# The last 96 hidden columns of a SwiGLU block: 64 of each weight in one product, 32 of each turned by DMA

## The chip, the cores and the metric

The kernel runs on one core of a Trainium2 chip. The core has a matrix engine (TensorE, PE in the profile, with its weight loads as PEld), VectorE (DVE), ScalarE (ACT), GpSimd (POOL) and a queue that issues DMAs (SyncE, SP); ScalarE's queue can issue DMAs too. The metric is device time in microseconds: the median of three runs of the kernel before is 252.13 us (251.43 to 252.75).

## The reference

The input x has 2048 tokens of 512 features, in bfloat16. Two branches are computed from it and mixed by a gate for each token:

```
g = sigmoid((x * gate_w).sum(-1))
a: q, k, v = x @ wqkv, 32 heads of 16; causal attention over the last 256 tokens; heads joined, @ wo
b: (silu(x @ w1) * (x @ w3)) @ w2            # w1, w3: 512 x 1376, w2: 1376 x 512
out = g * a + (1 - g) * b
```

The change is about branch b. Its hidden width is 1376 = 10 x 128 + 96, so that the last block of hidden columns is not full.

## The kernel before, in words

**Layout.** x lies turned in `xT` (features on partitions, four chunks of 128). Weights lie in `wqkv_sb`, `w1_sb`, `w3_sb`, `w2_sb` and `wo_sb`, loaded once. PSUM is used as one group of four banks, `su`, for attention scores and four single banks, `ch`, for everything else.

**Branch b.** For each of four blocks of 512 tokens (`tcb`) and each of eleven blocks of hidden columns (`f`, ten of 128 and one of 96), four products over the feature chunks give the gate part in one bank and four more the up part in another (`half`, L651). ScalarE takes the tanh of half the gate part (`th`, L656), VectorE makes from it, in two steps, silu(gate) times up (`m1`, L660 and `m2`, L665) and writes it to `hT`, hidden columns on partitions. Then for each of the block's four groups of 128 tokens eleven products with w2 (`part`, L702) give b, and VectorE scales it by 1 - g into `bsb` (`bev`, L707). The products stream 512 columns each; the block of 96 streams as many as a full one.

**Branch a.** For each quarter of the heads (`c`, 0 to 3) the projections (L374, L432) fill q, k and v; score batches (L493 near the diagonal, L525 and L533 far from it) go to `su`; ScalarE takes the exponential into `E` (L498, L540), VectorE and POOL mask it (L479, L552); p-v products of 34 columns (`pv`, L588) follow for each of 16 groups of tokens, VectorE normalises and gates them into `oc` (L596, L599), and a DMA issued by SP turns the tile into `OT` (`tr`, L605). When a group of tokens has all four quarters, four products with wo (`output`, L731) and one VectorE addition of `bsb` (L735) give the output, which SP stores (L740). The last group is done in two halves of 256 columns, the second stored from ScalarE's queue.

**Order.** The order is not written by hand. `Plan` holds every step with an engine, an assumed duration, what it depends on, the buffers it takes and frees, and a due time. `emit` goes through them as a list scheduler: it takes the engine that can start first, and of the steps that can start there at about the same time (a window of 0.005 us) the one with the earliest due time. `SLACK` is added to each step's end. Due times for attention come from `at(c, t)` with `T0` and `TA` and a lead for each kind; those of branch b are spread from `TF0` to `TF1` in proportion to the work; the output's are 8 us after `at(3, m)`. `landed` tells the planner when loads are there. The opening (`opening`, L255 to L282) is not planned: warm-up products, constants, and all loads in SP's queue, of which three times four turn x into `xT`. Each engine and each queue then carries out its own list in order, and waits at a step until what it needs is there.

**Names that the change touches.** `gw_turn` (L333) turns gate_w, which ScalarE's queue loads last into `gwr` (L264). `opening` and `constants4` set constants. `plan.pieces` splits a chain of four products into two steps, between which other work can be put.

## Time and profile before

| | |
|---|---|
| median of three runs | 252.13 us (251.43 to 252.75) |
| profiled execution, its own time | 251.68 us |
| its span, first to last instruction | 249.9 us |
| PE busy | 244.9 us (98%) |
| VectorE and ScalarE busy | 184.1 and 184.0 us (74%) |
| POOL busy | 107.4 us (43%) |
| products of the block of 96 (L651, 96 outputs) | 32 |
| turns of `oc` by DMA (L605) | 64, 2.3 us to landing (median) |

Groups carry the line of the kernel before. Durations of PE are modelled to the end of the pipeline, so one product of 512 columns is shown as 380 ns while the next starts 216 ns after it: what a stream costs is read from the chain in order of time, where pieces follow each other without overlap. SPq and ACTq rows are DMA issues; the time shown is that of the issue, not of the transfer. The granted TensorE clock was 1.00 in the whole execution.

### The profile page before, as it was taken

How to read it: one execution, taken by the hardware profiler on the slowest of the kernel's cores; microseconds unless marked ns; L12 is line 12 of the kernel's file. 1: busy time of each engine (PE TensorE's matmuls, PEld its weight loads, DVE VectorE, ACT ScalarE, POOL GpSimd, SP SyncE). 2: the span in 40 equal slices, each digit the busy share in tenths (PEclk: the TensorE clock that was granted, in tenths of full speed). 3: DMA queues.
4: the chain of work that ended last, by engine and by line, in shares of the span. 5: the costliest groups of instructions: out<-in, count | busy, mean ns of one | idle time of the engine just before them, and what ended most of it. 6: DMA issues, size and time to landing. Idle time of an engine off the chain costs nothing.

```text
span 249.9 us, 8005 instructions
## 1 busy us (share of the span) xinstructions
PE 244.9 (98%) x3434; PEld 132.9 (53%) x3434; DVE 184.1 (74%) x402; ACT 184.0 (74%) x181; POOL 107.4 (43%) x97
## 2 busy tenths in 40 slices
PE   7999999999999999999999999999999999999994
PEld 6545545555555455555455555545555546445452
DVE  5588978666877978775769887775669878786552
ACT  3579889687868988776788888766787774785521
POOL 7006560340808356391619174473538074150300
PEclk9999999999999999999999999999999999999999
DMA  7998950000000000000000000000000111111112
GB/s 212 314 266 253 221 116 18 13 5 13 8 18 6 13 14 11 16 8 13 5 18 13 13 7 13 14 11 13 8 18 26 55 29 54 34 50 32 50 34 68
DMA packets 28091, 13.14 MB, mean 53 GB/s; under 512 B 17336, under 2 KB 28056, under 8 KB 28056
## 3 DMA queue, kind: packets, MB, share of 16 engines
q1 hardware_dynamic: 27360, 12.17, 20.0%
q8 instruction: 27, 0.44, 0.8%
q10 hardware_dynamic: 696, 0.46, 0.6%
q14 instruction: 8, 0.07, 0.1%
HBM read 6.85 MB, written 2.10 MB: 36 GB/s over the span
## 4 chain that ended last, share of the span: by engine, by line
PE 93%; DMA 4%; DVE 1%; SPq 1%; issue 0%
PE ch L651 31%; PE ch L702 15%; PE ch L588 15%; PE ch L374 12%; PE su L493 8%; PE ch L432 6%; PE ch L731 5%; DMA OT<-oc 2%; PE su L525 2%; DMA w_sb<-in_B_w_dram 2%; DVE ot L735 1%; SPq L605 0%; DVE h L660 0%; SPq L249 0%; PE su L533 0%
## 5 line engine op out<-in xcount | busy, mean ns | idle before, releaser
L498 ACT ACTIVATE E<-su 128x2048 bf16<-128x2048 f32 x60 | 112.6, 1876 | 28.3 <-PE su L493 27.4
L552 POOL TENSOR_SCALAR_AFFINE_SELECT E<-E 64x1024 bf16<-64x1024 bf16 x56 | 65.1, 1162 | 119.2 <-ACT E L540 116.8
L651 PE MATMUL ch<-xT,w_sb 128*128 128x512 bf16 (+2 forms) x360 | 89.3, 375 | 0.4 <-DMA w_sb<-in_B_w_dram 0.4
L588 PEld LDWEIGHTS <-E 128*128 128x128 bf16 x1440 | 43.7, 96 | 12.3 <-issue 2.5
L651 PEld LDWEIGHTS <-w_sb 128*128 128x128 bf16 (+1 forms) x360 | 30.9, 99 | 31.0 <-issue 4.6
L588 PE MATMUL ch<-vbd,E 128*128 128x34 bf16 x1440 | 45.9, 178 | 0.0
L702 PE MATMUL ch<-w_sb,hT 128*128 128x512 bf16 (+1 forms) x176 | 44.0, 380 | 0.0
L479 DVE TENSOR_TENSOR E<-E,mdiag 128x512 bf16<-128x512 bf16 x64 | 33.7, 527 | 13.7 <-ACT E L498 13.3
L398 POOL TENSOR_SCALAR kbd<-kt,rowsA 128x512 bf16<-128x512 bf16 x24 | 37.5, 1573 | 6.8 <-DVE kt L395 5.5
L660 DVE SCALAR_TENSOR_TENSOR h<-tt,ch 128x512 bf16<-128x512 bf16 (+1 forms) x44 | 30.1, 685 | 12.6 <-ACT tt L656 12.0
L540 ACT ACTIVATE E<-su 128x2048 bf16<-128x2048 f32 (+1 forms) x16 | 26.6, 1663 | 12.6 <-PE su L525 7.9
L374 PE MATMUL ch<-xT,wqkv_sb 128*128 128x512 bf16 x128 | 34.1, 379 | 0.0
L665 DVE SCALAR_TENSOR_TENSOR hT<-h,ch 128x512 bf16<-128x512 bf16 (+1 forms) x44 | 30.2, 686 | 3.6
L656 ACT ACTIVATE tt<-ch 128x512 bf16<-128x512 f32 (+1 forms) x44 | 26.0, 594 | 6.8 <-PE ch L651 5.5
L599 DVE SCALAR_TENSOR_TENSOR oc<-ch,gq,rden 128x128 bf16<-128x128 f32 x64 | 22.4, 351 | 2.3
L493 PE MATMUL su<-qT,kbd 32*128 32x256 bf16 x480 | 23.9, 273 | 0.0
L702 PEld LDWEIGHTS <-hT 128*128 128x128 bf16 (+1 forms) x176 | 15.0, 97 | 16.3 <-issue 2.1
L596 DVE RECIPROCAL rden<-ch 128x8 f32<-128x8 f32 x64 | 13.1, 204 | 11.6 <-PE ch L588 10.7
L493 PEld LDWEIGHTS <-kbd 32*128 32x128 bf16 x480 | 7.1, 92 | 22.4 <-issue 21.8
L432 PEld LDWEIGHTS <-xT 128*128 128x128 bf16 x256 | 15.6, 97 | 4.6 <-issue 1.3
L731 PE MATMUL ch<-wo_sb,OT 128*128 128x512 bf16 (+1 forms) x68 | 16.6, 367 | 0.6 <-DMA OT<-oc 0.6
L374 PEld LDWEIGHTS <-wqkv_sb 128*128 128x128 bf16 x128 | 10.9, 97 | 11.3 <-issue 1.7
(54 smaller groups left out, 139.2 us busy)
## 6 DMA issues: line engine op xcount, KB each, us to landing
out_dram<-ot SPq DMA_DIRECT2D x15, 128.0 KB, 1.7
wqkv_sb<-in_A_wqkv_dram SPq DMA_DIRECT2D x6, 256.0 KB, 5.4
w_sb<-in_B_w_dram SPq DMA_DIRECT2D x1, 1280.0 KB, 6.5
w_sb<-in_B_w_dram SPq DMA_DIRECT2D x2, 608.0 KB, 5.9
w_sb<-in_B_w_dram SPq DMA_DIRECT2D x2, 512.0 KB, 5.5
OT<-oc SPq DMA_TRANSPOSE x64, 2.3
wo_sb<-in_A_wo_dram SPq DMA_DIRECT2D x1, 512.0 KB, 5.9
xs<-in_A_x_dram SPq DMA_DIRECT2D x1, 256.0 KB, 2.7
```

The costliest lines, as they stand in the source:

```text
L374: nc.tensor.matmul(pst[:], lhsT=wqkv_sb[:, dc, col + c * P:col + (c + 1) * P], rhs=xT[:, dc, tq * 512:(tq + 1) * 512], start=(dc == 0), st ...
L398: nc.gpsimd.tensor_scalar_mul(out=kv[:, :, h, :], in0=kt[kj.at["kt"]][:].rearrange("p (k t) -> p k t", t=KB), scalar1=rowsA[:, h:h + 1])
L432: nc.tensor.matmul(pst[:, mm * w:(mm + 1) * w], lhsT=xT[:, dc, m * P:(m + 1) * P], rhs=rhs, start=(dc == 0), stop=(dc == NDC - 1))
L479: nc.vector.tensor_tensor(out=e, in0=e, in1=mdiag[:, None, :].to_broadcast([P, 8, KB]), op=ALU.min)
L493: nc.tensor.matmul(su[:, s, par * 256:(par + 1) * 256], lhsT=kbd[r, 2 * t + par, :, :].rearrange("p a k -> p (a k)"), rhs=qT[r, q0:q0 + 25 ...
L498: nc.scalar.activation(out=E[ej.at["E"]][:, t % 4, :, :, 0:256], in_=su[:].rearrange("p s (a q) -> p s a q", a=2), func=ACT.Exp, scale=SCALE)
L552: nc.gpsimd.affine_select(out=e[lo:lo + KB], in_=e[lo:lo + KB], pattern=[[0, 16], [-1, KB]], compare_op=ALU.is_ge, fill=0.0, base=-1, chan ...
L588: nc.tensor.matmul(po[:, 34 * s:34 * s + 34], lhsT=e[:, off:off + P], rhs=vbd[:, 2 * t + par, s, :], start=(bi == 0), stop=(bi == len(bloc ...
L651: nc.tensor.matmul(ch[job.at["ch"]][0:fs, t0:t1], lhsT=w[:, dc, f * P:f * P + fs], rhs=xT[:, dc, tcb * 512 + t0:tcb * 512 + t1], start=(dc ...
L660: nc.vector.scalar_tensor_tensor(out=h1[job.at["h1"]][0:fs, :], in0=tt[job.at["tt"]][0:fs, :], scalar=1.0, in1=ch[job.at["ch"]][0:fs, :], ...
L665: nc.vector.scalar_tensor_tensor(out=hT[0:fs, f, :], in0=h1[job.at["h1"]][0:fs, :], scalar=0.5, in1=ch[up.at["ch"]][0:fs, :], op0=ALU.mult ...
L702: nc.tensor.matmul(bps[:], lhsT=hT[0:fs, f, mm * P:(mm + 1) * P], rhs=w2_sb[0:fs, f, :], start=(f == 0), stop=(f == NFC - 1))
```

## The change

**The 96 columns.** They are split into 64 and 32. For the 64, POOL copies w1's and w3's columns side by side into `wA`, and one chain of four products (`half` with `joint`) gives both gate and up, on partitions 0 to 63 and 64 to 127 of one bank. `th`, `m1` and `m2` then work on 64 partitions, with `m1` writing to the upper half.

For the 32, `wB` holds w1's and w3's columns, and `tail_columns` makes the products the other way round: tokens on partitions, x as the weight, 64 columns streamed, four chunks for each of four groups of 128 tokens, sixteen products. One tanh, and two VectorE steps over 4 x 32 columns, write the result into columns 64 to 95 of `hb`, which POOL has set to zero. Four DMAs on SP turn it, 128 x 128 each, into `hX`, so that the 32 columns come to lie on partitions 64 to 95. The joint block's `m2` waits for all four, and writes partitions 0 to 63 of `hX`; the value products read 96 partitions of it as the eleventh block. `hX` has two buffers, `hT` loses its eleventh block. `tail_columns` is put in ahead of the eighth of the eleven blocks.

**The end.** The output products of the last two groups of tokens are given as three products over the quarters 0 to 2 and one, later, over quarter 3. In the last half group, `bsb` is added on TensorE, by a product with the identity matrix, and ScalarE evicts the bank; the other half stays with VectorE.

**The plan.** `SLACK`, the window for equal starts, all due times and the assumed load times have other values. In the order as built, gate_w's turn stands on PE between the two halves of w1's first block, and both stand ahead of w3's; before, w3's first half came in between and gate_w's turn came after the second hidden block.

```diff
-SLACK = 0.08
+SLACK = 0.1039
...
-            rows = [r for r in lists[eng] if r[0] <= first + 0.005]
+            rows = [r for r in lists[eng] if r[0] <= first + 0.001]
...
+    FA = P // 2
+    FB = FL - FA
+    F0 = (NFC - 1) * P
...
-    hT = pp.tile([P, NFC, 512], BF16, name="hT")
+    hT = pp.tile([P, NFC - 1, 512], BF16, name="hT")
+    hX = pp.tile([P, 2, 512], BF16, name="hX")
+    wA = pp.tile([P, NDC, 2 * FA], BF16, name="wA")
+    wB = pp.tile([P, NDC, 2 * FB], BF16, name="wB")
+    tb = pp.tile([P, 4, FB], BF16, name="tb")
+    hb1 = pp.tile([P, 4, FB], BF16, name="hb1")
+    hb = pp.tile([P, 4, P], BF16, name="hb")
...
+        nc.gpsimd.memset(hb[:], 0.0)
...
-    T0, TA, TF0, TF1 = 10.0, 224.0, 0.0, 240.0
+    T0, TA, TF0, TF1 = 11.49, 234.3, -7.168, 250.6
...
-    landed = {"x": [4.0, 4.4, 15.6, 22.0, 30.0], "w13": [5.3, 5.8, 12.6, 19.8], "w2": 28.5,
-              "qkv": [6.6, 7.4, 8.2, 34.0], "wo": 31.5, "gw": 5.8}
+    landed = {"x": [3.7, 4.45, 15.4, 21.2, 30.2], "w13": [5.25, 6.15, 12.0, 18.7], "w2": 28.0,
+              "qkv": [7.1, 8.0, 8.8, 36.0], "wo": 32.0, "gw": 5.8}
...
-    a = add("PE", 0.1, gw_turn, [gw_in], 7.7, take=[(gjob, "ch")])
+    a = add("PE", 0.1, gw_turn, [gw_in], 9.407, take=[(gjob, "ch")])
...
-        lead = 18.0 if c else 3.0
+        lead = 9.235 if c else 0.5758
...
-        qdue = due if tq == 0 else at(c, 4 * tq - 4) - lead + 2.0
+        qdue = due if tq == 0 else at(c, 4 * tq - 4) - lead + 3.779
...
-        vdue = due + 1.5
+        vdue = due + 1.455
...
-        due = at(c, 4 * h) + 0.3
+        due = at(c, 4 * h) + 1.98
...
-        due = at(c, i) + -1.0
+        due = at(c, i) + 2.465
...
-    ffn_total = NTC * (NFC * 1.73 + 4 * 2.38)
+    ffn_total = NTC * ((NFC - 1) * 1.73 + 0.87 + 0.47 + 4 * 2.38)
...
+    w_ab = []
+    for dst, c0, src in ((wA, 0, w1_sb[:, :, F0:F0 + FA]), (wA, FA, w3_sb[:, :, F0:F0 + FA]),
+                         (wB, 0, w1_sb[:, :, F0 + FA:F]), (wB, FB, w3_sb[:, :, F0 + FA:F])):
+        def w_copy(dst=dst, c0=c0, src=src):
+            nc.gpsimd.tensor_copy(out=dst[:, :, c0:c0 + src.shape[2]], in_=src)
+
+        w_ab.append(add("POOL", 0.4, w_copy, [w13_in[3]], 22.0))
...
+        def tail_columns(tcb=tcb):
+
+            due = ffn_due(0.47)
+            job = Job()
+
+            def mm_b():
+                po = ch[job.at["ch"]]
+                for mm in range(4):
+                    m = 4 * tcb + mm
+                    for dc in range(NDC):
+                        nc.tensor.matmul(po[:, mm * 2 * FB:(mm + 1) * 2 * FB], lhsT=xT[:, dc, m * P:(m + 1) * P],
+                                         rhs=wB[:, dc, :], start=(dc == 0), stop=(dc == NDC - 1))
+
+            def cols(lo):
+                return ch[job.at["ch"]][:, 0:8 * FB].rearrange("p (m w) -> p m w", w=2 * FB)[:, :, lo:lo + FB]
+
+            def th_b():
+                nc.scalar.activation(out=tb[:], in_=cols(0), func=ACT.Tanh, scale=0.5)
+
+            def m1_b():
+                nc.vector.scalar_tensor_tensor(out=hb1[:], in0=tb[:], scalar=1.0, in1=cols(0),
+                                               op0=ALU.add, op1=ALU.mult)
+
+            def m2_b():
+                nc.vector.scalar_tensor_tensor(out=hb[:, :, FA:FL], in0=hb1[:], scalar=0.5, in1=cols(FB),
+                                               op0=ALU.mult, op1=ALU.mult)
+
+            a = add("PE", 0.47, mm_b, list(xt_ready[tcb]) + w_ab, due, take=[(job, "ch")])
+            a = add("ACT", 0.3, th_b, [a], due)
+            a = add("DVE", 0.25, m1_b, [a], due)
+            a = add("DVE", 0.25, m2_b, [a] + last_b, due, free=[(job, "ch")])
+            res = []
+            for mm in range(4):
+                def tr_b(mm=mm):
+                    nc.sync.dma_start_transpose(out=hX[:, tcb % 2, mm * P:(mm + 1) * P], in_=hb[:, mm, :])
+
+                res.append(add("SP", 1.1, tr_b, [a] + wx_done.get(tcb - 2, []), due, lat=1.3))
+            last_b[:] = res
+            return res
+
         for f in range(NFC):
-            fs = fsz(f)
-            due = ffn_due(1.73)
+            if f == NFC - 4:
+                turned = tail_columns()
+            joint = f == NFC - 1
+            due = ffn_due(0.87 if joint else 1.73)
             job = Job()
-
-            up = Job()
-
+            up = job if joint else Job()
...
+            def half(job, w, lo, hi, f=f, joint=joint, tcb=tcb, t0=0, t1=512):
                 for dc in range(lo, hi):
-                    nc.tensor.matmul(ch[job.at["ch"]][0:fs, t0:t1], lhsT=w[:, dc, f * P:f * P + fs],
+                    nc.tensor.matmul(ch[job.at["ch"]][:, t0:t1],
+                                     lhsT=wA[:, dc, :] if joint else w[:, dc, f * P:(f + 1) * P],
                                      rhs=xT[:, dc, tcb * 512 + t0:tcb * 512 + t1],
                                      start=(dc == 0), stop=(dc == NDC - 1))
 
...
+            rg = slice(0, FA if joint else P)
+            ru = slice(FA if joint else 0, P)
...
-            def m2(job=job, up=up, fs=fs, f=f):
-                nc.vector.scalar_tensor_tensor(out=hT[0:fs, f, :], in0=h1[job.at["h1"]][0:fs, :],
-                                               scalar=0.5, in1=ch[up.at["ch"]][0:fs, :],
+            def m2(job=job, up=up, rg=rg, ru=ru, f=f, joint=joint, tcb=tcb):
+                dst = hX[rg, tcb % 2, :] if joint else hT[:, f, :]
+                nc.vector.scalar_tensor_tensor(out=dst, in0=h1[job.at["h1"]][ru, :],
+                                               scalar=0.5, in1=ch[up.at["ch"]][ru, :],
                                                op0=ALU.mult, op1=ALU.mult)
...
-                                xt_ready[tcb] + win + last_up, due, [(job, "ch")])
-                b = plan.pieces(HALF, 0.2172, lambda lo, hi, half=half, up=up: half(up, w3_sb, lo, hi),
-                                [a], due, [(up, "ch")])
+                                xt_ready[tcb] + win + last_up + (w_ab if joint else []), due, [(job, "ch")])
+                b = a
+                if not joint:
+                    b = plan.pieces(HALF, 0.2172, lambda lo, hi, half=half, up=up: half(up, w3_sb, lo, hi),
+                                    [a], due, [(up, "ch")])
...
-            s1 = add("DVE", 0.69, m1, [t_], due, take=[(job, "h1")], free=[(job, "ch"), (job, "tt")])
-            s2 = add("DVE", 0.69, m2, [s1, b], due, take=[(hj, "hT")] if f == 0 else [],
-                     free=[(up, "ch"), (job, "h1")])
+            s1 = add("DVE", 0.69, m1, [t_], due, take=[(job, "h1")], free=[(job, "tt")] + ([] if joint else [(job, "ch")]))
+            s2 = add("DVE", 0.69, m2, [s1, b] + (turned if joint else []), due,
+                     take=[(hj, "hT")] if f == 0 else [], free=[(up, "ch"), (job, "h1")])
             if f:
                 s2.deps.append(hs[0])
             hs.append(s2)
...
+                    fs = P if f < NFC - 1 else FL
+                    ht = hT[:, f] if f < NFC - 1 else hX[0:FL, tcb % 2]
+                    nc.tensor.matmul(bps[:], lhsT=ht[:, mm * P:(mm + 1) * P],
                                      rhs=w2_sb[0:fs, f, :], start=(f == 0), stop=(f == NFC - 1))
...
-    def output(m, n0, n1, queue):
-        due = at(NDC - 1, m) + 8.0
+    def output(m, n0, n1, queue, late):
+        due = at(NDC - 1, m) + 19.44
         job = Job()
         part = n1 - n0
+        onto = queue == "ACT"
...
+        def onto_b():
+            nc.tensor.matmul(ch[job.at["ch"]][:, 0:part], lhsT=ident[:], rhs=bsb[:, m, n0:n1],
+                             start=False, stop=False)
+
         def oev():
-            nc.vector.tensor_tensor(out=ot[job.at["ot"]][:, 0:part], in0=ch[job.at["ch"]][:, 0:part],
-                                    in1=bsb[:, m, n0:n1], op=ALU.add)
+            dst = ot[job.at["ot"]][:, 0:part]
+            if onto:
+                nc.scalar.copy(out=dst, in_=ch[job.at["ch"]][:, 0:part])
+            else:
+                nc.vector.tensor_tensor(out=dst, in0=ch[job.at["ch"]][:, 0:part],
+                                        in1=bsb[:, m, n0:n1], op=ALU.add)
 
         def odma():
             eng = nc.sync if queue == "SP" else nc.scalar
             eng.dma_start(out=out2d[m * P:(m + 1) * P, n0:n1], in_=ot[job.at["ot"]][:, 0:part])
 
-        a = plan.pieces(HALF, 0.2172 * part / 512, omm, [ot_ready[(c, m)] for c in range(NDC)] + [wo_in], due,
-                        [(job, "ch")])
-        b = add("DVE", 0.69 * part / 512 + 0.02, oev, [a, b_ready[m]], due, take=[(job, "ot")],
-                free=[(job, "ch")])
+        each = 0.2172 * part / 512
+        if late:
+
+            a = add("PE", 3 * each, lambda: omm(0, NDC - 1),
+                    [ot_ready[(c, m)] for c in range(NDC - 1)] + [wo_in], due, take=[(job, "ch")])
+            if onto:
+                a = add("PE", each, onto_b, [a, b_ready[m]], due)
+            a = add("PE", each, lambda: omm(NDC - 1, NDC), [a, ot_ready[(NDC - 1, m)]], due)
+        else:
+            a = plan.pieces(HALF, each, omm, [ot_ready[(c, m)] for c in range(NDC)] + [wo_in], due,
+                            [(job, "ch")])
+        b = add("ACT" if onto else "DVE", 0.69 * part / 512 + 0.02, oev, [a] if onto else [a, b_ready[m]], due,
+                take=[(job, "ot")], free=[(job, "ch")])
         add(queue, 0.55, odma, [b], due, free=[(job, "ot")], lat=1.3)
 
     for m in range(NT - 1):
-        output(m, 0, D, "SP")
-    output(NT - 1, 0, D // 2, "SP")
-    output(NT - 1, D // 2, D, "ACT")
+        output(m, 0, D, "SP", m == NT - 2)
+    output(NT - 1, 0, D // 2, "SP", True)
+    output(NT - 1, D // 2, D, "ACT", True)
 
     with tc.manual_schedule():
         opening()
```

## The prediction

> **What bounds the kernel now.** I read first the page's busy times, then the chain that ended last, then the groups by shape, then PE's pieces in order of time.
>
> ```profile
> span 249.9 us, 8005 instructions
> PE 244.9 (98%) x3434; PEld 132.9 (53%) x3434; DVE 184.1 (74%) x402; ACT 184.0 (74%) x181; POOL 107.4 (43%) x97
> ...
> PE 93%; DMA 4%; DVE 1%; SPq 1%; issue 0%
> ```
>
> PE is busy all the time and carries 93% of the chain; VectorE and ScalarE have a quarter of the span free. A busy PE can hide gaps, so I priced the stream itself, from the chain in order of time:
>
> ```profile
> 7.60 1.73 PE ch L374 x8
> ...
> 44.09 0.59 PE ch L588 x24
> ...
> 64.70 0.89 PE ch L432 x16
> ...
> 240.29 1.20 PE ch L588 x48
> 241.49 0.89 PE ch L731 x4
> 242.40 0.70 DVE ot L735
> 243.10 0.64 SPq L605
> 243.84 2.32 DMA OT<-oc
> 246.21 0.73 PE ch L731 x5
> ```
>
> A product over 512 columns takes 1.73/8 = 216.2 ns, over 128 columns 0.89/16 = 55.6 ns, over 34 columns 0.59/24 = 24.6 ns. The first two lie on 1.9 ns + 0.418 ns per column (256: 109 ns, 64: 28.7 ns); 34 columns would be 16 ns by it, so 24.6 ns is a floor. A score batch (L493, L525) costs 0.43 us from stream to stream (in the timeline 0.33 from its first product to the next block's, and 0.1 ahead of it). Adding up PE's order of before with these prices, from 4.90 us on, puts the end of the last p-v product at 239.79 us; the profile has it at 241.49 us. The difference is nearly all in four places: 0.8 us at the opening, 0.25 near 26 us, 0.17 near 205 us, 0.5 near 226 us. So before is PE's sum plus about 1.7 us, and then a fixed tail of 8.4 us (241.49 to 249.9) set by the last turned tile: its DMA lands at 246.16, eight products of 256 columns follow, two additions, the store. The reader should see in the last five rows that at the end the chain leaves PE, and goes through the issue (SPq) and landing (DMA) of one turned tile.
>
> The opening, in the timeline (PE only waits there for w3's first columns), and SP's queue behind it:
>
> ```profile
> 2.00 0.62 ACTq L264 DMA_DIRECT2D gwr<-in_gate_w_dram  x1
> 5.14 0.60 PE L651 MATMUL ch<-xT,w_sb 128*128 128x256 bf16 x4
> 6.12 1.48 PE L651 MATMUL ch<-xT,w_sb 128*128 128x256 bf16 x12 [0.38 <-DMA w_sb<-in_B_w_dram]
> ```
> ```profile
> 29.03 2.05 SPq L605 DMA_TRANSPOSE OT<-oc  x1
> 31.18 1.18 SPq L605 DMA_TRANSPOSE OT<-oc  x1
> 32.45 1.18 SPq L605 DMA_TRANSPOSE OT<-oc  x1
> 33.73 2.36 SPq L605 DMA_TRANSPOSE OT<-oc  x1
> 36.18 1.18 SPq L605 DMA_TRANSPOSE OT<-oc  x1
> ```
>
> SP issues loads until 28.9 us; then the turns that have queued up go out one behind the other, 1.2 us each and now and then 2.05 to 2.4.
>
> **Products of the 96 columns.** Removed: per 512 tokens eight 512-column products (two blocks of 96 outputs); added: four such (64 columns of w1 and of w3 side by side) and sixteen of 64 columns. Over four blocks: 16 x 216.2 = 3.46 us off, 64 products on. The trace has none of 64 columns with a 128-column weight; the nearest rows bound one at 24.6 and 55.6 ns, 1.57 to 3.56 us in all. I take 28.7 ns, the line through the two longer rows, as it lies above the floor: 1.84 us. One 256-column product (bsb through the identity) adds 0.11. PE's sum: -3.46 + 1.84 + 0.11 = -1.51 us.
>
> Here a page speaks against the change. Every added product loads its own weight, and the PEld row has 97 ns for such a load (L432) while the stream advances 55.6 ns: loads overlap. The Trainium skill, "TensorE: Matmul & The Clock Gate", section "Back-to-back issue gap", gives a stream of load and product about 81 ns at 128 columns; the trace disagrees (55.6 ns), and its floor of about 25 ns for 1 to 64 columns agrees with 24.6. By 81 ns each the 64 would be 5.2 us and the whole sum +1.8 us.
>
> **VectorE, ScalarE, POOL.** Added: eight products-with-scalar over 128 columns on VectorE, which I bound by the reciprocal of 8 columns (0.20) and the 512-column row (0.69); I take 0.25: 2 us. ScalarE gets four tanh of 128 columns (0.17 to 0.59; 0.3 taken) and the last half eviction. POOL gets one memset (half of the 0.95 us one) and four copies at 22 us: 512 elements take 1.57 us there, so 256 and 128 take 0.8 and 0.4, 2.4 us together, done by about 21 us if w3's last columns land at 18.3 (issue 12.40 plus 5.9); their first reader on PE is due at about 24. All of it costs nothing while VectorE and ScalarE are a quarter idle; without that cover it would be 2 and 1.5 us.
>
> **Sixteen turns on SP.** In the built order the first chunk's four stand in SP's queue as 3rd, 4th, 5th and 7th behind the loads, that is behind 29.03 us. By the rows above they issue at 32.45, 33.73, 36.18 and about 38.7 (37.5 if no long issue falls among them), and a turn lands 2.3 us after issue: 39.8 to 41.0, or 42.3 with one more long issue. The second multiplication of the joint block (L732 of the changed file) waits for all four, and VectorE is in order: behind it stand a reciprocal and normalisation, a mask and a bsb scaling, and on PE the hX product and the value product that takes its bank. Its operands are ready at about 40.0 (joint product ends at 37.1, the exponential ahead of it on ScalarE at 38.5, tanh 0.6, mask and first multiplication 1.2), and PE reaches the hX product at 41.66, so a landing up to 40.9 is free. Bounds 0 to 1.5 us; I take 0.45. In the later chunks the turns have 11 to 16 us between the 64-column products and the joint block and cost nothing; in the fourth they stand ahead of the turn of p-v tile 5, which has 6.4 us until its output product: about 5.3 us of issues behind 203.5, then 2.3 to land, still covered by a microsecond. If it were not, PE would wait as it does at 226 us (0.5).
>
> **Opening.** gate_w's turn now stands ahead of the second half of w1's first block, and that half ahead of w3's. Four 256-column products (0.44) move into the wait that ends at 6.12. The landing of gwr is not in the trace: issued at 2.00, behind a load whose first reader starts at 5.14. If it lands by 5.7, -0.45; if it is the last to land, 0. I take -0.45, since 1 KB directly behind that load should follow it closely.
>
> **New order of the rest.** All due times change. Score batches stay 2.75 us or more apart in both orders (shortest 2.58 and 2.56 by the count), and p-v to output product is at least 4.0 us apart now against 3.4 to 3.6 before, where the waits at 205 and 226 us arose. I take these 0.67 us as gone. New waits elsewhere: the spacing shows none, and the bounds are 0 and 1.5 us (as many as before had); I take 0.
>
> **The end.** Of PE's -1.51, 1.2 us is work taken out from behind the last p-v product (3.8 instead of 4.97 us), where it only filled the wait for the turned tile; ahead of it the sum falls by 0.32. Behind the landing stand two 256-column products in place of eight, and the two halves are evicted side by side (ScalarE, VectorE) instead of in sequence: from 246.21 the last eviction ends after 0.8 instead of 1.17 us: -0.38. Two turns back to back took 2.13 and 1.19 us at 241.6; a short one would give another 1 us.
>
> **Sum** against the profiled execution (251.68 us: span 249.9 and 1.8 around it): -0.32 - 0.45 - 0.67 + 0.45 - 0.38 = -1.37, so 250.3 us. That execution was 0.45 us under the median of 252.13, so I forecast 250.8 us.
>
> **Rivals.**
> 1. The turns land in time and the last two issue quickly: another -0.45 and up to -1.0, 249.4 us. For it: most single turns issue in 1.09 us. Against: two of the four that took over 2 us are in SP's backlog, and one is the last but one. Chance 0.18.
> 2. The new order brings waits of its own of about 1 us: 251.8 us, no change to be told. For it: before had four such places. Against: PE's count shows no shortfall. Chance 0.17.
> 3. Slower: the first chunk's turns all issue at 2.36 us. The last is then issued at 43.5, lands at 45.8, the joint block's result is there at 46.5, PE stands 4.9 us: 252.13 - 1.82 + 4.9 = 255.2 us. It decides from a landing at 42.8 on, 1.9 us past the free point. Against it: the backlog's first five average 1.6 us. Chance 0.11.
> 4. The 64-column products run at the pace of their weight loads (97 ns each, 6.2 us, +4.4): 255.2 us. The 34-column stream at 24.6 ns with the same loads speaks against it. Chance 0.03. The Trainium skill's 81 ns ("TensorE: Matmul & The Clock Gate", section above) would give a milder form of it, +3.3 us and 254.1 us, and falls by the same rows.
>
> **How the numbers follow.** Forecast 0.51 (249.8 to 251.7), rivals 0.18, 0.17, 0.11, 0.03. Half a per cent, 1.26 us, is about what a measurement can tell from no change; the forecast lies just beyond it, so three quarters of its chance count as faster and one quarter as same, rival 1 as faster, rival 2 as same. Faster 0.56, same 0.29, slower 0.15. The range from 249.2 to 252.3 takes in forecast and rivals 1 and 2 and leaves out 3 and 4.
>
> **What would show it.** Right: 64-column products near 29 ns apart; joint second multiplication in the first chunk waiting under 1 us for a turn; the first f-block done by 7.1 us; last p-v product ending near 240.5; under 8.1 us from there to the end. Wrong: PE idle for microseconds at about 42 us, the 64-column products at 55 ns or more, or waits of PE in the new order that before did not have.

## The result

The changed kernel takes 251.25 us (median; 250.81 to 252.22), the kernel before, run beside it, 251.74 us. The ratio is 0.9974 [0.9962, 0.9986]: faster by a quarter of a per cent, half of what the prediction called measurable. The time lies 0.45 us above the forecast of 250.8 and inside its range, about midway between the forecast and rival 2 (251.8). That is not because the sum was right: it had a gain of 1.37 us, and the spans of the two profiled executions differ by 0.5. Four of its terms missed by 0.45 to 1.1 us each, in both directions, and 0.9 us of the misses did not cancel. The distance to the forecast is smaller than that because the forecast was taken from 252.13 us, three runs of the kernel before, which runs at 251.74 here; that is luck.

The profiled execution of the changed kernel took 251.17 us. The page:

```profile
span 249.4 us, 8138 instructions
PE 244.4 (98%) x3483; PEld 133.8 (54%) x3483; DVE 187.4 (75%) x409; ACT 185.4 (74%) x186; POOL 109.2 (44%) x102
...
PE 94%; DVE 2%; DMA 1%; ACT 1%; issue 0%; SPq 0%; DVEq 0%
```

PE is as busy as before, although work was taken from it. In the shares of the chain ScalarE's 1% is new, VectorE has gone from 1% to 2%, and DMA from 4% to 1%. The chain in order of time (start, length, what) says where:

```profile
4.11 1.71 PE ch L319 x16
...
93.43 1.89 ACT E L505
95.34 1.18 DVE E L486
96.52 0.61 DVE h L726
97.17 0.76 PE ch L595 x24
...
111.38 1.28 DVE E L486
...
142.45 0.45 PE ch L439 x8
142.91 0.47 PE ch L672 x16
...
243.63 2.23 DMA OT<-oc
```

Three things are to be seen. The first row is the turning of x at the opening: 16 products of 128 columns at 107 ns, twice the 55.6 ns that they take later (0.45/8 = 56 ns in the row at 142.45). At 93 to 97 and at 111 us the chain leaves PE for a mask of VectorE (L486), which lasts 1.2 to 1.3 us there; the same instruction takes 0.42 us in most places. And sixteen 64-column products (L672) take 0.47 us, 29 ns each.

The end, in the timeline:

```profile
240.69 1.36 PE L595 MATMUL ch<-vbd,E 128*128 128x34 bf16 x48
...
245.91 0.39 PE L804 MATMUL ch<-wo_sb,OT 128*128 128x256 bf16 x2 [0.28 <-DMA OT<-oc]
246.28 0.42 DVE L816 TENSOR_TENSOR ot<-ch,bsb 128x256 bf16<-128x256 f32 x1 [0.36 <-PE ch L804]
246.34 0.37 ACT L814 CAST ot<-ch 128x256 bf16<-128x256 f32 x1 [2.47 <-PE ch L804]
246.74 0.39 ACTq L821 DMA_DIRECT2D out_dram<-ot  x1
```

Before, five products stood behind the last turned tile, and the two halves were evicted one behind the other by VectorE:

```profile
246.21 0.72 PE L731 MATMUL ch<-wo_sb,OT 128*128 128x256 bf16 x5 [0.27 <-DMA OT<-oc]
...
246.58 0.81 DVE L735 TENSOR_TENSOR ot<-ch,bsb 128x256 bf16<-128x256 f32 x2 [0.24 <-PE ch L731]
```

Only two products of 256 columns stand there now, and the halves are evicted side by side.

The account between the two profiled executions uses PE's sum at the prediction's prices, laid against the real starts of the 76 score batches; where the distance between the two grows, PE waited. (The bracket of a timeline row gives about 0.3 us less for the same wait, because it starts at the modelled end of the product before.)

| | before | after | difference |
|---|---|---|---|
| PE's sum from 4.90 us to the last p-v product | | | -0.32 |
| distance at the first score batch (opening) | 0.79 | 1.25 | +0.46 |
| distance gained from there to the last batch (waits) | 1.03 | 1.46 | +0.43 |
| last p-v product's end to the end of the span | 8.4 | 7.35 | -1.05 |
| sum; the spans give 249.4 - 249.9 = -0.5 | | | -0.48 |

### The profile page after: what moved, and what is told of

It is laid out like the page before. It is cut to its first block, busy times and chain, and to the rows that moved or that the text cites. A ratio compares the mean times of both kernels' runs of the same rounds, so it can differ in the third digit from the quotient of the medians.

```text
span 249.4 us, 8138 instructions
## 1 busy us (share of the span) xinstructions
PE 244.4 (98%) x3483; PEld 133.8 (54%) x3483; DVE 187.4 (75%) x409; ACT 185.4 (74%) x186; POOL 109.2 (44%) x102
## 4 chain that ended last, share of the span: by engine, by line
PE 94%; DVE 2%; DMA 1%; ACT 1%; issue 0%; SPq 0%; DVEq 0%
PE ch L712 29%; PE ch L773 15%; PE ch L595 15%; PE ch L381 11%; PE su L500 8%; PE ch L439 6%; PE ch L804 5%; PE su L532 2%; PE su L260 1%; DVE E L486 1%; DMA OT<-oc 1%; PE ch L672 1%; ACT E L505 1%; PE ch L319 1%; DVE oc L606 0%
## 5 line engine op out<-in xcount | busy, mean ns | idle before, releaser
L505 ACT ACTIVATE E<-su 128x2048 bf16<-128x2048 f32 x60 | 112.6, 1877 | 28.7 <-PE su L500 27.8
L559 POOL TENSOR_SCALAR_AFFINE_SELECT E<-E 64x1024 bf16<-64x1024 bf16 x56 | 65.0, 1161 | 84.7 <-ACT E L547 82.3
L712 PE MATMUL ch<-xT,w_sb 128*128 128x512 bf16 (+1 forms) x328 | 79.5, 375 | 0.0
L405 POOL TENSOR_SCALAR kbd<-kt,rowsA 128x512 bf16<-128x512 bf16 x24 | 37.6, 1578 | 27.3 <-DVE kt L402 23.3
L595 PE MATMUL ch<-vbd,E 128*128 128x34 bf16 x1440 | 46.6, 178 | 0.5 <-DVE E L486 0.3
L712 PEld LDWEIGHTS <-w_sb 128*128 128x128 bf16 x328 | 28.3, 98 | 29.8 <-issue 3.6
L486 DVE TENSOR_TENSOR E<-E,mdiag 128x512 bf16<-128x512 bf16 x64 | 34.8, 544 | 9.1 <-ACT E L505 7.7
L773 PE MATMUL ch<-w_sb,hT 128*128 128x512 bf16 x160 | 41.3, 379 | 0.0
L726 DVE SCALAR_TENSOR_TENSOR h<-tt,ch 128x512 bf16<-128x512 bf16 (+1 forms) x44 | 30.1, 684 | 6.4 <-ACT tt L722 5.7
L732 DVE SCALAR_TENSOR_TENSOR hT<-h,ch 128x512 bf16<-128x512 bf16 x40 | 27.5, 687 | 3.8
L773 PEld LDWEIGHTS <-hT 128*128 128x128 bf16 x160 | 13.1, 97 | 13.0 <-issue 1.9
```

What stands on the lines that cost most here:

```text
L405: nc.gpsimd.tensor_scalar_mul(out=kv[:, :, h, :], in0=kt[kj.at["kt"]][:].rearrange("p (k t) -> p k t", t=KB), scalar1=rowsA[:, h:h + 1])
L486: nc.vector.tensor_tensor(out=e, in0=e, in1=mdiag[:, None, :].to_broadcast([P, 8, KB]), op=ALU.min)
L505: nc.scalar.activation(out=E[ej.at["E"]][:, t % 4, :, :, 0:256], in_=su[:].rearrange("p s (a q) -> p s a q", a=2), func=ACT.Exp, scale=SCALE)
L559: nc.gpsimd.affine_select(out=e[lo:lo + KB], in_=e[lo:lo + KB], pattern=[[0, 16], [-1, KB]], compare_op=ALU.is_ge, fill=0.0, base=-1, chan ...
L595: nc.tensor.matmul(po[:, 34 * s:34 * s + 34], lhsT=e[:, off:off + P], rhs=vbd[:, 2 * t + par, s, :], start=(bi == 0), stop=(bi == len(bloc ...
L712: nc.tensor.matmul(ch[job.at["ch"]][:, t0:t1], lhsT=wA[:, dc, :] if joint else w[:, dc, f * P:(f + 1) * P], rhs=xT[:, dc, tcb * 512 + t0:t ...
```

## Experiments

### Each part of the change alone

Theory A: the split of the 96 columns brings its gain by itself. Theory B: it is the order that the planner makes from it, with its new due times, that decides.

The first kernel has the split with the plan's numbers and the end as before:

```diff
-SLACK = 0.1039
+SLACK = 0.08
-    T0, TA, TF0, TF1 = 11.49, 234.3, -7.168, 250.6
+    T0, TA, TF0, TF1 = 10.0, 224.0, 0.0, 240.0
...   (all other due times, leads and load times too; output() as before)
```

> The 96 columns as in the changed kernel, but the plan's numbers and the output end as before. If the parts add up as the prediction has them, PE's stream loses 1.6 us and the time falls by 1.2 to 1.6 us against before, with the last p-v product that much earlier. If the gain of the split is given back by waits of whatever order the planner makes of it, the time falls by under 0.5 us and PE's idle places have grown by about a microsecond.

The second has the kernel before with the new end only (`output` with `late`, the addition of `bsb` on PE, ScalarE's eviction):

```diff
-    def output(m, n0, n1, queue):
+    def output(m, n0, n1, queue, late):
...
-    output(NT - 1, 0, D // 2, "SP")
-    output(NT - 1, D // 2, D, "ACT")
+    output(NT - 1, 0, D // 2, "SP", True)
+    output(NT - 1, D // 2, D, "ACT", True)
```

> Before with the output end of the changed kernel alone (last two groups in three and one products, last half added on TensorE and evicted by ScalarE; due times as before). By the prediction's working the stretch from the last landing to the end shortens by 0.38 us and PE's sum grows by 0.11: about -0.4 us. The rival, that the end is set by the issue and landing of the last turns alone, gives 0 to -0.1.

The third has the kernel before with the new numbers of the plan only:

```diff
-SLACK = 0.08
+SLACK = 0.1039
-    T0, TA, TF0, TF1 = 10.0, 224.0, 0.0, 240.0
+    T0, TA, TF0, TF1 = 11.49, 234.3, -7.168, 250.6
...   (and all other numbers of the change)
```

> Before with the plan's numbers of the changed kernel alone (slack, window, due times, assumed load times). By the prediction the opening gains 0.45 us and the waits near 205 and 226 us go (0.67): about -1 us. If instead the new order brings waits of its own (masks on VectorE that come late to a p-v product, seen at 97 and 112 us in the changed kernel) and the opening gains nothing when the matrix engine's clock comes late, it is 0 to +0.8 us.

The fourth is the changed kernel with the numbers of before, that is split and end together:

```diff
-SLACK = 0.1039
+SLACK = 0.08
...   (all numbers as in the first; output() as changed)
```

> The changed kernel with all of the plan's numbers as before. If the new numbers are worth the 1 us that the prediction gave them, this is slower than the changed kernel by about that, -0.4 to -0.8 us against before. If they cost what they bring or more, it is as fast as the changed kernel or faster: -0.7 to -1.6 us against before.

| split | end | plan | median, us | ratio to before |
|---|---|---|---|---|
| yes | no | no | 253.25 | 1.0056 [1.0026, 1.0085] |
| no | yes | no | 252.99 | 1.0028 [0.9999, 1.0056] |
| no | no | yes | 255.13 | 1.0123 [1.0082, 1.0164] |
| yes | yes | no | 252.70 | 1.0037 [1.001, 1.0064] |
| yes | no | yes | 251.29 | 0.9991 [0.9978, 1.0004] |
| yes | yes | yes | 251.25 | 0.9974 [0.9962, 0.9986] |

(The fifth row is the last but one experiment, below; end and plan without the split was not run.) No part alone gains, and the plan's numbers alone cost most; split and plan together have nearly the whole gain. For the split alone five of the twelve runs had a granted clock of 0.991 or 0.992 and took 254.1 to 254.6 us; the median of the other seven is 252.89 us, still slower than the kernel before beside it (251.93). The split takes 1.62 us out of PE's sum, as counted; in its order, PE's waits grow by 1.53 us at 39 and 0.55 us at 83 us, and from the last p-v product to the end it takes 9.6 us where the kernel before takes 8.4. The plan's numbers alone bring waits of 1.34, 0.84 and five of 0.4 to 0.6 us. All four kernels of the first four rows came out slower than either theory of their expectations had them.

The new end by itself shows a second effect. The timeline of that kernel:

```profile
246.65 0.28 PE L732 MATMUL ch<-wo_sb,OT 128*128 128x256 bf16 x1
246.77 0.81 PE L702 MATMUL ch<-w_sb,hT 128*128 128x512 bf16 x3
247.62 0.69 ACT L709 ACTIVATE bsb<-ch,omg 128x512 bf16<-128x512 f32 x1 [7.88 <-PE ch L702]
248.34 0.42 DVE L744 TENSOR_TENSOR ot<-ch,bsb 128x256 bf16<-128x256 f32 x1 [1.83 <-ACT bsb L709]
248.36 0.27 PE L736 MATMUL ch<-bsb,ident 128*128 128x256 bf16 x1 [0.78 <-ACT bsb L709]
```

The last turned tile is there at 246.6, but value products of branch b still stand on PE, and the eviction of the last group's `bsb` starts only at 247.62: b ends the kernel, not the turned tile. In the kernel before that eviction started at 244.78. The split with the old plan ends the same way, with the old end and with the new one. So with the old plan the new end doesn't set the end; which of the plan's new numbers it takes wasn't tried.

### Whose waits: POOL's far masks left out

In the changed kernel the two largest waits lie near 97 and 112 us. The timeline of the first:

```profile
92.70 4.83 POOL L559 TENSOR_SCALAR_AFFINE_SELECT E<-E 64x1024 bf16<-64x1024 bf16 x4 [1.25 <-ACT E L547]
...
95.34 1.18 DVE L486 TENSOR_TENSOR E<-E,mdiag 128x512 bf16<-128x512 bf16 x1 [0.70 <-ACT E L505]
...
96.44 0.67 DVE L726 SCALAR_TENSOR_TENSOR h<-tt,ch 128x512 bf16<-128x512 bf16 x1
...
97.17 0.76 PE L595 MATMUL ch<-vbd,E 128*128 128x34 bf16 x24 [0.23 <-DVE h L726]
```

While POOL works through four far masks (its masks on E, L559), VectorE's diagonal mask takes 1.18 instead of 0.42 us; the multiplication behind it in VectorE's list ends at 97.1, and PE's p-v product needs the bank that it frees. Theory: a mask that meets a POOL instruction is held up by it. Rival: it is slow or late for another reason, and the order alone makes the wait. Three kernels leave out POOL's far masks (and with them a part of the attention mask), with all orders kept:

```diff
-            for lo in (0, KB):
-                nc.gpsimd.affine_select(out=e[lo:lo + KB], in_=e[lo:lo + KB],
-                                        pattern=[[0, 16], [-1, KB]],
-                                        compare_op=ALU.is_ge, fill=0.0, base=-1, channel_multiplier=1)
+            return
```

On the changed kernel:

> The changed kernel, its order untouched, with POOL's far masks left out (part of the attention mask is then missing). Theory: VectorE's diagonal mask stands still while a POOL far mask runs (1.1 to 1.35 us in place of 0.42), VectorE's list slips, and PE waits for a mask or a bank: 0.6 us at 97 us and 0.45 at 112 us. Then the slow masks and those two waits go and the time falls by 0.9 to 1.2 us against the changed kernel (about -1.6 us against before). Rival: VectorE's list is too dense there whatever POOL does; then the waits stay and the time is that of the changed kernel.

On the split alone:

> The split of the 96 columns alone, in the order of the plan's numbers of before, with POOL's far masks left out. Theory: its waits of 1.5 us near 38 us and 0.55 us near 82 us, both behind a slow diagonal mask, go, and the gain of PE's sum comes through: 2 us less than with the far masks, about -0.7 us against before. Rival (the order is bad in itself, or the first chunk's turns set the wait): still +1 us or more against before.

On the kernel before, as control:

> Control: the kernel before with POOL's far masks left out. Its own waits (opening, 0.25 near 27 us, 0.5 near 227 us) stand behind DMAs, not behind masks, so theory expects 0 to -0.4 us. If leaving the far masks out takes as much here as in the two others, the masks cost every order the same and do not tell the orders apart.

| far masks left out of | median, us | ratio to before | waits of PE at these places |
|---|---|---|---|
| changed kernel | 249.91 | 0.9927 [0.9914, 0.9941] | both gone |
| split alone | 251.30 | 0.9974 [0.9963, 0.9986] | 1.53 falls to 0.88, 0.55 goes |
| kernel before | 251.61 | 0.9999 [0.9986, 1.0011] | (not there) |

VectorE's masks were nearly as slow in the kernel before. Its group, and that of the changed kernel (busy, mean ns, idle before):

```profile
L479 DVE TENSOR_TENSOR E<-E,mdiag 128x512 bf16<-128x512 bf16 x64 | 33.7, 527 | 13.7 <-ACT E L498 13.3
```
```profile
L486 DVE TENSOR_TENSOR E<-E,mdiag 128x512 bf16<-128x512 bf16 x64 | 34.8, 544 | 9.1 <-ACT E L505 7.7
```

Without far masks the mean is 436 ns in the first of the three kernels and 432 in the third. In the changed order leaving them out gains 1.3 us (251.25 to 249.91); in the order of before the ratio shows nothing. That nothing isn't quite one: the three kernels without far masks spend about 2.0 us outside the span from first to last instruction, all others 1.7 to 1.8. By the medians of the spans the gain is 1.65 us in the changed kernel (249.55 to 247.9) and 0.45 us in the kernel before (250.1 to 249.65), and by the count PE's waits fall to 0.15 us in both profiled executions, from 1.46 and 1.03. So leaving out the far masks gains in both orders, and over three times as much in the new one: how much a held-up mask costs depends on whether PE at once needs what stands behind it. For the split alone most of the loss goes too, but 0.88 us of the first wait stays.

### POOL's instructions in halves

Here the whole computation is kept; each far mask and each k mask of POOL (L405, which fills `kbd`) is issued as two of half the size, in the same order:

```diff
-            e = E[ej.at["E"]][:, 2 * i:2 * i + 2, :, :, 256:320].rearrange("p t s a q -> p (t s a) q")
             for lo in (0, KB):
-                nc.gpsimd.affine_select(out=e[lo:lo + KB], in_=e[lo:lo + KB],
-                                        pattern=[[0, 16], [-1, KB]],
-                                        compare_op=ALU.is_ge, fill=0.0, base=-1, channel_multiplier=1)
+                for t in (2 * i, 2 * i + 1):
+                    e = E[ej.at["E"]][:, t, :, :, 256:320].rearrange("p s a q -> p (s a) q")
+                    nc.gpsimd.affine_select(out=e[lo:lo + KB], in_=e[lo:lo + KB],
+                                            pattern=[[0, 8], [-1, KB]],
+                                            compare_op=ALU.is_ge, fill=0.0, base=-1, channel_multiplier=1)
...
+                for k0 in (0, 4):
                     nc.gpsimd.tensor_scalar_mul(
-                    out=kv[:, :, h, :], ...
+                        out=kv[:, k0:k0 + 4, h, :], ...
```

On the changed kernel:

> The changed kernel, its order untouched, with each POOL far mask and each POOL k mask done as two of half the size. If VectorE's mask stands still for as long as one POOL instruction lasts, no diagonal mask takes over about 1 us any more, the waits at 97 and 112 us shrink by half or go, and the time falls by 0.4 to 1.0 us against the changed kernel. If VectorE waits for the whole run of POOL work, or slows by sharing, nothing changes, or POOL's longer total (some 20 us more) costs time.

250.05 us, ratio 0.9921 [0.9905, 0.9937]. The same place in its timeline:

```profile
92.84 5.50 POOL L562 TENSOR_SCALAR_AFFINE_SELECT E<-E 64x512 bf16<-64x512 bf16 x8 [0.74 <-ACT E L549]
...
95.47 0.42 DVE L488 TENSOR_TENSOR E<-E,mdiag 128x512 bf16<-128x512 bf16 x1 [0.69 <-ACT E L507]
...
95.95 0.69 DVE L729 SCALAR_TENSOR_TENSOR h<-tt,ch 128x512 bf16<-128x512 bf16 x1
...
96.90 0.76 PE L598 MATMUL ch<-vbd,E 128*128 128x34 bf16 x24
```

The mask starts at nearly the same point beside the same run of POOL's masks, but 0.04 us ahead of one of the halves and no longer 0.23 us into a whole one; it takes 0.42 us, and PE waits for nothing. Over the whole kernel, by groups (busy, mean ns, idle before):

```profile
L562 POOL TENSOR_SCALAR_AFFINE_SELECT E<-E 64x512 bf16<-64x512 bf16 x112 | 74.0, 683 | 75.1 <-ACT E L549 64.4 <-PE ch L598 8.3
...
L488 DVE TENSOR_TENSOR E<-E,mdiag 128x512 bf16<-128x512 bf16 x64 | 28.8, 449 | 9.6 <-ACT E L507 8.2 <-ACT E L555 0.9
```

POOL pays 16 us more (109.2 to 125.0), 9 of them for the far masks (65.0 to 74.0, two times 683 ns for one of 1161), and no wait of PE leads to it; the masks' mean falls from 544 to 449 ns, and PE's waits by the count from 1.46 to 0.14 us. This kernel is faster than both others. Far masks and k masks were not halved one without the other.

On the kernel before, as control:

> The kernel before, with each far mask and each k mask of POOL as two instructions of half the size; orders of all engines unchanged. Theory A (a mask of VectorE that is blocked by a long POOL instruction costs time only where PE's next product waits for what stands behind it, and the order of before has no such place): ratio 0.998 to 1.001, 251.4 to 252.1 us, PE's waits at 26.8, 207 and 227 us as before. Theory B (shorter POOL instructions are worth what they were worth in the changed kernel whatever the order, 0.9974 to 0.9921): ratio about 0.995, 250.6 us.

251.06 us, ratio 0.9976 [0.9963, 0.9989]: between the two theories, nearer to theory A by the time, and against it by the waits. Halving helps before too, by half of what it gives the changed kernel; PE's waits, 1.03 us before, sum to 0.1. So the statement that before had no place where a held-up instruction costs time is too strong. The timeline of the kernel before shows such a place:

```profile
202.53 1.19 DVE L479 TENSOR_TENSOR E<-E,mdiag 128x512 bf16<-128x512 bf16 x1 [1.56 <-ACT E L498]
...
204.41 0.69 DVE L665 SCALAR_TENSOR_TENSOR hT<-h,ch 128x512 bf16<-128x512 bf16 x1
...
205.16 1.02 PE L651 MATMUL ch<-xT,w_sb 128*128 128x512 bf16 x4
```

The mask takes 1.19 us, the second multiplication behind it, which frees a bank, ends at 205.10, and PE's next products start at 205.16, 0.17 us late by the count. The wait of 0.25 us near 26 us stands in the same way behind a mask of 0.87 us (23.55). The one near 226 us stands behind a turned tile, which lands 3.54 us after its issue with the halves in place of 3.85; why is open. With halves on both sides the change is worth 1.0 us by the medians (251.06 - 250.05) and 1.4 us by the ratios (0.9921/0.9976 = 0.9945), about twice what it is worth without.

On the split alone:

> The split alone (the kernel of 253.25 us, ratio 1.0056, with waits of 1.53 us at 39.2 and 0.55 us at 82.7), with POOL's far masks and k masks in halves; whole computation kept. Theory A (both waits are VectorE's masks blocked by POOL's long instructions): both waits fall below 0.4 us, 251.0 to 251.6 us, ratio 0.9965 to 0.999. Theory B (the first wait comes from something else in VectorE's list, as 0.88 us of it stayed when the far masks were left out): about 0.9 us stays there, 251.7 to 252.2 us, ratio 0.999 to 1.001.

251.35 us, ratio 0.9977 [0.9959, 0.9996]: the time that theory A gave, but by the waits theory B holds for the first place. The second wait went; of the first, 1.28 of 1.53 us stayed, by the count. Its timeline:

```profile
33.89 1.88 ACT L507 ACTIVATE E<-su 128x2048 bf16<-128x2048 f32 x1 [0.37 <-PE su L502]
...
35.80 0.89 DVE L488 TENSOR_TENSOR E<-E,mdiag 128x512 bf16<-128x512 bf16 x1 [0.77 <-ACT E L507]
...
36.61 0.74 DVE L390 TENSOR_SCALAR kbd<-ch,rowsA 128x512 bf16<-128x512 f32 x1
...
37.27 0.67 DVE L729 SCALAR_TENSOR_TENSOR h<-tt,ch 128x512 bf16<-128x512 bf16 x1
...
38.00 0.76 PE L598 MATMUL ch<-vbd,E 128*128 128x34 bf16 x24 [0.99 <-DVE h L729]
```

The mask stands ahead of two steps that free banks, and VectorE waits 0.77 us for ScalarE's exponential before it; then all three run one behind the other while PE stands. This same mask takes 1.13 us in the split alone, 0.89 with the halves and 0.42 without far masks, and the bracket before the p-v product reads 1.24, 0.99 and 0.54 us: PE's wait changes by what the mask changes. So the held-up mask is 0.70 of the 1.24 us and the order the rest. My reading that both waits of the split alone are held-up masks was right for a little over half of this one.

### The end and the opening by themselves

The changed kernel with the end as it was:

```diff
-    def output(m, n0, n1, queue, late):
+    def output(m, n0, n1, queue):
...   (body and calls as before; due time 19.44 kept)
```

> The changed kernel with the end as it was before (eight products of the last half tile behind its turn, both additions on VectorE). Theory A (the prediction's end term): 0.38 us slower than the changed kernel, from the last landing to the last eviction 1.17 us in place of 0.80; 251.5 to 251.8 us, ratio 0.9985 to 1.0005. Theory B (the new end is worth nothing, as it was worth nothing when put into the kernel before by itself, 1.0028): 251.2 us, ratio 0.9974.

251.29 us, ratio 0.9991 [0.9978, 1.0004]. The medians put it 0.04 us from the changed kernel, the ratios 0.17% (0.4 us); the intervals overlap, and the time does not tell the theories apart. The timeline supports the mechanism: from the last turned tile's first product (245.74) to the end of the last eviction (246.93) it is 1.19 us, against 0.80 in the changed kernel (245.91 to 246.71). PE's start was 0.35 us earlier in this execution, which hides it in the span.

The changed kernel with w1, w3, w1, w3 at the opening, as before, and gate_w's turn behind them (the numbers are those of the plan's steps: 872 to 875 the block's halves, 25 and 26 gate_w's turn and its eviction, 876 the tanh):

```diff
+        was = [872, 25, 874, 26, 873, 876, 875]
+        new = [872, 873, 874, 875, 25, 26, 876]
+        at = {op.seq: n for n, (est, op) in enumerate(order)}
+        row = {op.seq: (est, op) for est, op in order}
+        for a, b in zip(was, new):
+            order[at[a]] = row[b]
         self.order = order
```

> The changed kernel with one edit in the opening: the first hidden block's halves in the order of before (w1, w3, w1, w3), gate_w's turn behind them; all else in the same order. Theory A (the prediction's opening term: w1's second half fills the wait for w3's first columns): 0.45 us slower than the changed kernel, 251.7 us, ratio 0.9992, and PE waits 0.3 to 0.5 us for w3 ahead of the second group of four products. Theory B (what the new order saves at w3 it gives back, since the first products run at half pace and w3 has landed by then, or since gate_w is waited for): 251.0 to 251.4 us, ratio 0.9965 to 0.998.

251.38 us, ratio 0.9993 [0.998, 1.0007]: by the medians it is 0.13 us slower than the changed kernel, as theory B has it, and by the ratio it is where theory A has it, so the time does not tell them apart. The timelines show why the gain can't be relied on. In this kernel PE waits for w3:

```profile
6.43 1.48 PE L718 MATMUL ch<-xT,w_sb 128*128 128x256 bf16 x12 [0.45 <-DMA w_sb<-in_B_w_dram]
```

and in the kernel with the plan's numbers alone, which has the new order, for gate_w, until much the same time:

```profile
6.30 0.17 PE L334 MATMUL ch<-ident,gwr 4*128 4x4 bf16 x1 [0.54 <-DMA gwr<-in_gate_w_dram]
```

In the changed kernel without far masks PE waits for gate_w until 6.22. So the new order trades one wait for another. And where the first products run slowly for long (the row of 16 products shown in the next section lasts 1.73 to 1.91 us in five of the 14 profiled executions, the changed kernel's among them) PE waits for neither load; in the other nine it waits 0.24 to 1.79 us for one of them.

## Why the prediction was right, and where it was wrong

**PE's sum: right.** 64-column products take 29.4 ns (0.47/16), against 28.7 taken and bounds of 24.6 and 55.6; no weight load shows in them. Rival 4 falls, in its milder form too. The split alone gives -1.62 us, and the whole change -1.51 us, by the count at these prices.

**VectorE, ScalarE, POOL at nothing: right for the added work, wrong in the reason.** The copies on POOL take 0.40 and 0.29 us, the new steps of VectorE 0.28 us, and no wait leads to them. But "a quarter idle" was no proof of cover: VectorE's list is carried out in order, and the mask at 95.34 us, which ends 0.76 us late, puts the steps behind it late, whatever idle time follows.

**First chunk's turns: taken at 0.45, worth 0.** The last issue came at 38.41, close to the 38.7 forecast, and its tile was there at 40.86, inside the 39.8 to 41.0 given. From two windows of the changed kernel's timeline:

```profile
38.41 1.23 SPq L696 DMA_TRANSPOSE hX<-hb  x1
```
```profile
40.86 0.69 DVE L732 SCALAR_TENSOR_TENSOR hX<-h,ch 64x512 bf16<-64x512 bf16 x1 [0.16 <-DMA hX<-hb]
```

VectorE waits 0.16 us and PE not at all: PE reaches the hX product only at 42.22, not at 41.66, most of it because of the slower opening. A landing up to 40.9 was called free, and 40.86 was. Rival 3, the slow side, needed a landing at 42.8, 1.9 us later.

**Opening: wrong, -0.45 for about 0, and +0.46 in the profiled execution.** The step that failed is the choice "I take -0.45, since 1 KB directly behind that load should follow it closely": where PE waits for gate_w, it does so until 6.22 and 6.30 us, not 5.7. The bound at 0 was the right end. On top of it came the pace of the first products, which differs from one profiled execution to the next, whatever the kernel:

```profile
3.90 1.10 PE L312 MATMUL ch<-ident,xs 128*128 128x128 bf16 x16
```
```profile
3.90 1.91 PE L319 MATMUL ch<-ident,xs 128*128 128x128 bf16 x16
```

The first is of before, the second of after; two experiments with the order of before at the opening (the new end alone, before with halves) also have 1.91. The Trainium skill ("TensorE: Matmul & The Clock Gate", Part 1) says that the clock doubles after a free-running window, so that the point of change wanders; the traces agree in the two paces, 107 and 56 ns, and in the wandering. The profile's row of granted clock is the same in both, with the highest digit in every slice, so only the durations tell. It is not the change's doing: in the ten profiled executions whose traces hold every product, the distance at the first score batch is 0.9 to 1.4 us in the four with the new order of the opening and 0.8 to 2.3 in the six with the old one, and that of before is the smallest of all. The 0.46 us of the account is therefore chance.

**Waits gone, -0.67, and new ones, 0: wrong.** This is the step that failed most. The wait of 0.5 us near 226 us did go, and so did the smaller one near 205, which the prediction put down to the spacing of p-v and output product and which, by the times above, stood behind a held-up mask. But the order has new ones of 0.58 and 0.45 us near 97 and 112 and four smaller: 0.43 us more in all than before, where the prediction had 0.67 less. It searched for them in the spacing of score batches and of output products on PE (and gave two figures for the least spacing of batches, 2.75 and about 2.57 us), and not in what stands behind each mask in VectorE's list. The bounds, 0 to 1.5 us, held it. Rival 2 named the result ("waits of its own of about 1 us") and not the mechanism, which the runs show: VectorE's mask under one of POOL's far masks takes up to three times as long; with the far masks left out, or with POOL's instructions halved, mask and waits shrink together. One of the prediction's own signs of being wrong, "waits of PE in the new order that before did not have", came about, and two of its signs of being right did not: the first hidden block was done at 7.9 us and not by 7.1, and the last p-v product ended at 242.05 and not near 240.5.

**The end, -0.38: right in its mechanism and more came.** From the first product on the last turned tile to the last eviction it is 0.80 instead of 1.17 us, as predicted. (The prediction counted eight products there before; its own row shows five. The time was read from the evictions and stands.) The rest of the -1.05 came ahead of the landing: the last two turns were issued within 2.61 us, not 3.41, which rival 1 had priced with up to 1.0. Before and after:

```profile
241.61 3.41 SPq L605 DMA_TRANSPOSE OT<-oc  x2
```
```profile
242.11 2.61 SPq L612 DMA_TRANSPOSE OT<-oc  x2
```

This goes with the split and not with end or plan: the eight other kernels with the split have 2.61 to 2.63 us, the five without it, before among them, 3.03 to 3.41. What sets it wasn't tried.

So both halves of rival 1 happened (turns in time, last turns quick); with 1.1 us beyond the sum they paid for about half of what the waits and the opening cost against it, 2.0 us. Taken singly, the rivals were treated as alternatives; they were separate steps, and the first two came about together.

## What to carry to other kernels

An engine with a quarter of its span free can still set the pace for a moment: for each step that is priced at nothing because its engine is idle, look at the order behind it, and ask who waits if one instruction in front takes three times as long. When two engines work on the same kind of buffer, compare the longest instance of a group with its median before an order is changed; if long ones coincide with the other engine's instructions, make those shorter, which here gained 1.2 us for two edits and no change of order, and 0.7 us in the kernel before. A due-time table fits the work that it was made for: put into another kernel it cost 1.2%, so a change of work and of plan should be tried together and judged together.

## What was not expected of the hardware

The mask of VectorE (two bf16 operands in SBUF, 128 x 512) takes 0.41 to 0.43 us in the 36 of its 64 cases in the changed kernel that start while POOL is idle. The 16 that start under a far mask of POOL (1.14 to 1.23 us) all end 0.27 us after that far mask ends, wherever in it they started, and so take 0.47 to 1.35 us; in the kernel before 15 of 16 do the same. The multiplications with one operand in PSUM (L726) don't show it: the 18 that start under a far mask take 0.67 to 0.69 us like the others. The Trainium skill ("SBUF — State Buffer", section "Who interferes with whom") states that VectorE and GpSimd share a port pair under an exclusive lock, that an instruction of VectorE with two inputs in SBUF contends there with one of GpSimd that reads SBUF, and, for VectorE's two-port modes, that the first to issue has the pair for its whole instruction. For the far masks the trace agrees, as at the second wait:

```profile
111.23 1.14 POOL L559 TENSOR_SCALAR_AFFINE_SELECT E<-E 64x1024 bf16<-64x1024 bf16 x1
...
111.30 1.35 DVE L486 TENSOR_TENSOR E<-E,mdiag 128x512 bf16<-128x512 bf16 x1
...
112.70 0.67 PE L595 MATMUL ch<-vbd,E 128*128 128x34 bf16 x20 [0.28 <-DVE E L486]
```

The far mask ends at 112.38 and the mask at 112.65. For POOL's k masks, which read SBUF as well, "the whole instruction" does not hold. Eleven of the 12 masks that start under one take 0.41 to 0.43 us, as here:

```profile
157.08 1.56 POOL L405 TENSOR_SCALAR kbd<-kt,rowsA 128x512 bf16<-128x512 bf16 x1
...
157.65 0.42 DVE L486 TENSOR_TENSOR E<-E,mdiag 128x512 bf16<-128x512 bf16 x1
```

The twelfth, which starts 0.33 us into its k mask, takes 0.64 and ends 0.96 us after the k mask's start. In all profiled executions the masks that a whole k mask slows end at 0.96 to 0.97 us from its start, as if it held VectorE for its first 0.7 us only (an estimate: 0.96 less the 0.27 of above).

A shorter far mask then means a shorter hold: with the halves no diagonal mask takes more than 0.71 us, and one that starts in the gap between two halves, like that at 95.47 us, isn't held at all. The lock itself is the skill's explanation and was not tried otherwise.
